# Attention with bucket masks and two expert layers on one core: the first heads' v halves, one conversion and many places moved

## Chip, core and metric

One core of a Trainium2 chip runs the whole program. The metric is device time in microseconds (us) from launch to end of that core. Its engines are TensorE (PE, matmuls; PEld is its weight load), VectorE (DVE), ScalarE (ACT), GpSimd (POOL) and the sync engine (SP), which here only issues transfers (DMAs). A time "of the profile" is measured from the first instruction of one profiled execution.

## What is computed

```python
# q, k, v: (2, 8, 768, 64): 16 heads (h) of 768 rows and 64 columns
q_bucket, k_bucket = bits of (q @ proj > 0), (k @ proj > 0)      # 6 bits each
mask = q_bucket[:, None] == k_bucket[None, :]
scores = where(mask, q @ k.T / 8, -1e9)
attn = softmax(scores);  x = attn @ v                            # -> x: 1536 tokens x 512
h = x @ w_in                     # layer 1: 512 -> 2048
g = (a0 + a1 h + a2 h^2 + a3 h^3) / (1 + |b0||h| + |b1| h^2 + 1e-6)
x = g @ w_out                    # 2048 -> 512
h = x @ w2_in;  out = (h - tanh(h)) @ w2_out                     # layer 2
```

## The kernel before

Numbers of 32 bits are carried through TensorE as two halves (a rounded high part and the rest), so most products are three matmuls. The program has two stages.

The **attention stage** handles 16 heads, each in six chunks j of 128 keys. Per head: `load_qk` brings k and q in one tile (kq); `split_hi` (ScalarE) and `split_lo` (GpSimd, for head 0 VectorE) make the halves A and Bl; `place` and its second part copy them by DMA into the operand tiles TA, TBk and TBq; `bits` multiplies them by the projection (six matmuls in PSUM) and its second part turns the signs into mask rows of TBk and TBq on VectorE, followed by one DMA (head 0 writes both directly). `smax` multiplies for the row maxima, and VectorE reduces them (line 380, mx); `put_max` (head 0: `put_half`, twice) transposes them and sends them as one more row of TBq by DMA. `scores` needs that row: four matmuls (line 498, st), then Exp on ScalarE (e), `round_e` rounds e to 16 bits (eh; `EH_ACT` says how many of 768 columns ScalarE takes, VectorE the rest), `rest_e` subtracts (el; GpSimd, in the last head also VectorE by `EL_DVE_LAST`), and `attend` multiplies eh and el with v (pv). For each pair of heads v is loaded (vraw), its maximum found (`vmax` on VectorE, `vall` on TensorE, "vback" on VectorE, "vagain" on TensorE, `vscale` on VectorE) and each head's v is split into `vhi` (ScalarE) and `vlo` (line 473); `vmean_of` needs both. `normalize` and, for every second head, `to_x` (xT, then xh and xl) write the next stage's input.

Into the last heads the program threads the first eight conversions of the weights (`load_w`, `scale` on ScalarE, `join` on VectorE with two instructions and a PSUM tile "low", `halves` on ScalarE and GpSimd) and the first unit of the expert layer (four `h_mm` with stages a to e).

The **expert stage** then runs on TensorE as a row of 48-matmul blocks: `h_mm` (line 171) and `y_mm` (lines 687, 691) alternately. Its PSUM tiles take over the banks of the attention stage, each as soon as that bank's last user is done.

The order is written out by hand. Every call is entered as a task with a "place"; head h has the base 6h, and a value of the table T, or of EARLY for heads 0 to 3, is added. The tasks are sorted by place and emitted, and **every engine, SP too, runs its instructions in exactly this order**. So a changed number in T matters only where it makes two tasks change sides. The large PSUM tiles (bits, sm, st, xT, low, early h) share three slots of two banks ("double"); the small ones (maxima, v's maximum, mean) share one bank ("single").

Of the kernel before, what the change touches and what calls it, by code (L numbers as in the profile page):

```python
# [10 lines left out]
F32, F32R, F16, I32 = DT.float32, DT.float32r, DT.float16, DT.int32  # L11
AF = mybir.ActivationFunctionType
ALU = mybir.AluOpType
AX = mybir.AxisListType
PSUM = bass.MemoryType.PSUM

B, H, S, D = 2, 8, 768, 64
# [3 lines left out]
P = 128  # L21
NK = S // P
SH = S // 2
# [4 lines left out]
PW = D + 1  # L28


EH_ACT = (768, 768, 384, 768, 512, 768)
ORDERED = ('scalar', 'vector', 'gpsimd', 'tensor', 'sync')
TC_ARGS = dict(schedule_with_timeline_sim=True)
M = dict(a=1, b=3.35, c=3.69, d=5, e=5, y=1.59, scale=3.71, join=3.82, halves=6.35)
EH_ACT_LAST = (0, 0, 768, 0, 384, 0)
EL_DVE_LAST = (128, 0, 0, 128, 256, 384)

EL_DVE = (0, 0, 0, 0, 0, 0)


T = dict(load=-22.01, hi=-15.34, lo=-14.2, place=-13.97, place_a=-13.59, bits=-13.42, bits_out=-12.57,
         put=-3.25, put_out=-3.12, vhi=-6.87, vlo=-4.93, vmean=-2.03, vmean_out=-1.18, lead=9.98, max=0.3,
         exp=0.13, round=0.9, rest=1.95, pv=(5.43, 6.95, 7.43, 8.75, 8.06, 9.23), pv_last=(5.5, 5.5, 7.19,
         8.17, 8.91, 9.32), norm=9.74, x=14.29, x_out=15.02, v=-16.67, vmax=-11.5, vall=-10.2, vscale=-9.9,
         w=-24, w_step=3.88, h0=0.75, slot=0.88, a=0.84, b=2.13, c=2.55, d=4.03, e=4.18, gates=26.99,
         vback=-10.1, vagain=-9.93, w2=-8.0, w2_step=4.0, w_load=6.0)
EARLY = {0: dict(load=-61, hi=-59.04, lo=-59.03, place=-57.89, bits=-57.11, bits_out=-56.82, place_a=-56.45,
                lead=54.43, put=-49.1, v=-59.99, vmax=-57.43, vall=-55.7, vscale=-55.6, vhi=-4.1, vlo=-4.02,
                vmean=-2.21, vmean_out=-1.2, vback=-55.67, vagain=-55.64, put_half=-51.0),
         1: dict(load=-66.5, hi=-64.64, lo=-64.4, place=-61.82, bits=-59.23, bits_out=-58.61, place_a=-57.18,  # L50
                lead=53.53),
         2: dict(load=-64.71, hi=-60, lo=-59.75, place=-59.59, place_a=-59.53, bits=-56.42, bits_out=-56.02,
                lead=9.98, v=-22.32),
         3: dict(load=-20, hi=-15.31, lo=-14.17, place=-14.21, place_a=-13.68, bits=-12.43, bits_out=-11.41,
                lead=9.23)}
NE = 1
T_LAST = dict(norm=9.59, x=10.17, x_out=10.68)


@with_exitstack  # L60
def tile_fn(ctx: ExitStack, tc: tile.TileContext, kq, v, proj, w1i, w1o, a_, b_, w2i, w2o, out):
    nc = tc.nc
# [112 lines left out]
    NCH, NG, FG = 3, 4, 4  # L175
# [66 lines left out]
    with ExitStack() as actx:  # L242
        actx.enter_context(tc.manual_schedule(engines={getattr(nc, e).engine for e in ORDERED}))
        ap = actx.enter_context(tc.tile_pool(name="ap", bufs=1))
# [11 lines left out]
        def halved(x):  # L256
            return x.rearrange("p (n c) ... -> p n c ...", n=2)
# [12 lines left out]
        TAk, TAq, TBk, TBq = {}, {}, {}, {}  # L270
        raw, hilo = {}, {}

        def after(what):

            return nullcontext()
# [8 lines left out]
        praw = ap.tile([P, NB], F32, name="praw")  # L284
# [11 lines left out]
        thr = ap.tile([P, 1], F32, name="thr")  # L296
        amp = ap.tile([P, 1], F32, name="amp")
# [5 lines left out]
        nc.vector.tensor_add(amp, amp, th2)  # L303
        pj = ap.tile([P, P], F32, name="pj")
        nc.vector.memset(pj, 0.0)
        nc.vector.tensor_copy(pj[0:D, 64:70], praw[0:D])
        nc.vector.tensor_scalar(pj[0:D, 70:76], praw[0:D], -1.0, None, op0=ALU.mult)
        nc.vector.tensor_scalar(pj[D:P, 96:102], praw[D:P], -1.0, None, op0=ALU.mult)
        nc.vector.tensor_copy(pj[D:P, 102:108], praw[D:P])
        pj_hi = ap.tile([P, P], F32R, name="pj_hi")  # L310
        pj_lo = ap.tile([P, P], F32R, name="pj_lo")
        nc.vector.tensor_copy(pj_hi, pj)
# [34 lines left out]
        def bits(h):  # L347
            hi, lo = hilo.pop(h)
            ps = double(f"bits{h}")[:, :, 0:SH]
            for x, (l, r) in enumerate(((pj_hi, hi), (pj_lo, hi), (pj_hi, lo))):  # L350
                for n in range(2):
                    nc.tensor.matmul(ps[:, n], l, r[:, n * SH:(n + 1) * SH], start=(x == 0), stop=(x == 2))  # L352

            def out():
                if h == 0:
                    nc.vector.tensor_scalar(halved(TBq[h][64:76]), ps[96:108], thr[96:108], amp[96:108],
                                            op0=ALU.is_gt, op1=ALU.mult)
                    nc.vector.tensor_scalar(halved(TBk[h][64:77]), ps[64:77], thr[64:77], amp[64:77],
                                            op0=ALU.is_gt, op1=ALU.mult)
                    return  # L360
                d = nc.vector.tensor_scalar(halved(TBk[h][64:108]), ps[64:108], thr[64:108], amp[64:108],  # L361
                                            op0=ALU.is_gt, op1=ALU.mult)
                sent.setdefault("thr", d.ins)
                d = nc.sync.dma_start(TBq[h][64:76].bitcast(F32), TBk[h][96:108].bitcast(F32))
                sent.setdefault("bits", d.ins)

            outs["bits", h] = out
# [38 lines left out]
        vraw, vsc, vmx = {}, {}, {}  # L406

        def vsl(h):
            return vraw[h // 2][:, :, (h % 2) * D:(h % 2 + 1) * D]
# [6 lines left out]

        def vmax(pr):
            vmx[pr] = ap.tile([P, 2], F32, name=f"vm{pr}", tag="vm", bufs=2)
            with after("max" if pr else "thr"):
                nc.vector.tensor_reduce(vmx[pr], vraw[pr].rearrange("p t (h d) -> p h t d", h=2),  # L420
                                        axis=AX.XY, op=ALU.max, apply_absolute_value=True)

        nc.vector.memset(pj, 1.0)
        ones2 = pj[0:2]
# [45 lines left out]

        def vlo(h):
            t = VB[h % 3]
            nc.vector.scalar_tensor_tensor(out=t[:, :, D + 1:2 * D + 1], in0=vsl(h), scalar=vsc[h],  # L473
                                           in1=t[:, :, 0:D], op0=ALU.mult, op1=ALU.subtract)

# [44 lines left out]
        pv = {}  # L520
# [72 lines left out]
        def on(place, fn, *args):  # L593
            tasks.append((place, len(tasks), fn, args))

        end, TT = 6 * BH, globals()["T"]
        for h in range(BH):
            g, last = 6 * h, h == BH - 1
            T = {**TT, **EARLY.get(h, {})}
            if h > 0:  # L600
                on(g + T["load"], load_qk, h)
            on(g + T["hi"], split_hi, h)
            on(g + T["lo"], split_lo, h)
            on(g + T["place"], place, h)
            on(g + T["bits"], bits, h)
            on(g + T["place_a"], out_of, "place", h)
            on(g + T["bits_out"], out_of, "bits", h)
            if h:
                on(g + T["put"], put_max, h)
                on(g + T["put_out"], out_of, "put", h)  # L610
            else:
                on(g + T["put_half"], put_half, 0)
                on(g + T["put"], put_half, NK // 2)
            on(g + T["vhi"], vhi, h)
            on(g + T["vlo"], vlo, h)
            on(g + T["vmean"], vmean_of, h)
            on(g + T["vmean_out"], out_of, "vmean", h)
            for j in range(NK):
                on(g + j - T["lead"], smax, h, j)
                on(g + j - T["lead"] + T["max"], out_of, "max", (h, j))  # L620
                on(g + j, scores, h, j)
                on(g + j + T["exp"], out_of, "e", (h, j))
                on(g + j + T["round"], round_e, h, j)
                on(g + j + T["rest"], rest_e, h, j)
                on(g + (T["pv"] if not last else T["pv_last"])[j], attend, h, j)
            t = T if not last else T_LAST
            on(g + t["norm"], normalize, h)
            if h % 2 == 0:
                on(g + T["v"], load_v, h // 2)
                on(g + T["vmax"], vmax, h // 2)  # L630
                on(g + T["vall"], vall, h // 2)
                on(g + T["vback"], out_of, "vback", h // 2)
                on(g + T["vagain"], out_of, "vagain", h // 2)
                on(g + T["vscale"], vscale, h // 2)
            else:
                on(g + t["x"], to_x, h // 2)
                on(g + t["x_out"], out_of, "x", h // 2)
        for n, p in enumerate((f, part) for part in range(2) for f in range(FG)):
            t = end + (TT["w"] + TT["w_step"] * n if n < FG else TT["w2"] + TT["w2_step"] * (n - FG))
            on(t - TT["w_load"], load_w, *p)  # L640
            on(t, W1.scale, *p)
            on(t + 1, W1.join, *p)
            on(t + 2, W1.halves, *p, nc.gpsimd)
        for u in range(NE):
            for fi in range(FG):
                t = end + TT["h0"] + TT["slot"] * (4 * u + fi)
# [74 lines left out]
    for u in range(NU):  # L721
        t = 8 * u
# [68 lines left out]
```

## Time and profile before

| | us |
|---|---|
| median of 3 runs | 786.19 (782.45 to 789.7) |
| the profiled execution, whole | 783.02 |
| its span, first to last instruction | 781.2 |
| TensorE busy | 745.8 (95% of the span) |
| VectorE, GpSimd, ScalarE busy | 525.8, 507.0, 466.2 |

The profile lists each engine's busy time, what ended the idle time before an instruction ("<-"), and the granted clock of TensorE (PEclk; 1.00 is full). A stage in which TensorE is never idle can only be shortened by less work for it; in the others the time hangs on what TensorE waits for.

### The profile page before, as it was taken

What the parts mean: (1) busy time and instruction counts of PE and PEld (TensorE: products, weight loads), DVE (VectorE), ACT (ScalarE), POOL (GpSimd) and SP (SyncE); (2) the same over time, 40 slices, a digit from 0 to 9 for tenths busy, and PEclk for the clock granted to TensorE, in tenths of its full rate; (3) what the DMA queues carried; (4) which work ended last, traced back from release to release, by engine and by line L of the source; (5) the groups of instructions that cost most, each with busy time, mean ns of one, the idle gap of its engine ahead of it and who ended that gap; (6) DMA issues with size and microseconds to landing.
All of it is one profiled execution on the core that took longest, in us unless ns stands there. A gap on an engine that the chain in (4) does not pass through costs nothing.

```text
span 781.2 us, 13222 instructions
## 1 busy us (share of the span) xinstructions
PE 745.8 (95%) x5081; PEld 627.9 (80%) x5081; DVE 525.8 (67%) x820; ACT 466.2 (60%) x756; POOL 507.0 (65%) x395
## 2 busy tenths in 40 slices
PE   4799999999899699999999999999999999999998
PEld 3689888888787588888888888888888888888886
DVE  6678988898879888879899898853322444342222
ACT  2388888878796788777666676764444333332120
POOL 2298898988889687787777778985333434342221
PEclk9999999999999999999999999999999999999999
DMA  6564546447421231121222211221221212200012
GB/s 169 159 164 129 136 135 166 127 112 193 119 77 61 62 101 55 55 80 56 59 76 76 61 54 56 74 86 55 71 64 55 82 54 60 77 27 1 28 41 95
DMA packets 40536, 66.49 MB, mean 85 GB/s; under 512 B 3844, under 2 KB 26468, under 8 KB 40472
## 3 DMA queue, kind: packets, MB, share of 16 engines
q1 hardware_dynamic: 40472, 65.63, 28.8%
q8 instruction: 40, 0.66, 0.4%
q14 instruction: 24, 0.20, 0.1%
HBM read 43.00 MB, written 3.15 MB: 59 GB/s over the span
## 4 chain that ended last, share of the span: by engine, by line
PE 82%; DVE 12%; ACT 2%; issue 2%; DMA 1%; SPq 0%; ACTq 0%; DVEq 0%
PE h L171 32%; PE y L691 17%; PE y L687 17%; PE st L498 6%; DVE mx L380 4%; PE sm L376 3%; PE bits L352 2%; DVE eh L509 1%; PE pv L536 1%; DVE VB L473 1%; PE pv L537 1%; PE pv L539 1%; DVE TBk L361 1%; ACT e L501 1%; DMA vraw<-in_v_dram 1%
## 5 line engine op out<-in xcount | busy, mean ns | idle before, releaser
L239 POOL TENSOR_TENSOR G<-g,G 128x512 fp32r<-128x512 f32 x96 | 123.4, 1295 | 119.5 <-ACT G L234 104.6
L518 POOL TENSOR_TENSOR el<-e,eh 128x768 f16<-128x768 f32 (+2 forms) x96 | 159.1, 1673 | 33.0 <-ACT eh L507 20.2
L171 PE MATMUL h<-xh,wh 128*128 128x512 f32 x368 | 144.0, 391 | 3.6 <-DVE wt L110 3.6
L171 PE MATMUL h<-xl,wh 128*128 128x512 f32 x368 | 143.7, 390 | 0.0
L171 PE MATMUL h<-xh,wl 128*128 128x512 f32 x368 | 143.7, 390 | 0.0
L122 POOL TENSOR_TENSOR wl<-wt,wh 128x512 fp32r<-128x512 f32 x64 | 83.6, 1306 | 71.7 <-ACT wh L121 71.1
L687 PE MATMUL y<-G,wh 128*128 128x512 f32 x384 | 118.3, 389 | 0.0
L691 PE MATMUL y<-wh,G 128*128 128x512 f32 x384 | 118.1, 389 | 0.0
L234 ACT CAST G<-g 128x512 fp32r<-128x512 f32 x96 | 58.3, 619 | 84.9 <-PE y L691 35.7
L501 ACT ACTIVATE e<-st,lnk 128x768 f32<-128x768 f32 x96 | 86.2, 899 | 31.7 <-PE st L498 28.3
L110 DVE SCALAR_TENSOR_TENSOR wt<-wt,low 128x512 int32<-128x512 int32 x64 | 44.0, 687 | 89.5 <-ACT wt L98 85.2
L704 DVE TENSOR_TENSOR ya<-y,ya 128x512 f32<-128x512 f32 x72 | 49.1, 688 | 77.8 <-PE y L691 72.7
L380 DVE TENSOR_REDUCE mx<-sm 128x1 f32<-128x768 f32 x96 | 90.7, 951 | 12.7 <-PE sm L376 10.7
L171 PEld LDWEIGHTS h<-xh,wh 128*128 128x128 f32 x368 | 69.5, 189 | 18.2 <-issue 3.8
L691 PEld LDWEIGHTS y<-wh,G 128*128 128x128 f32 x384 | 72.1, 188 | 14.9
L687 PEld LDWEIGHTS y<-G,wh 128*128 128x128 f32 x384 | 72.1, 188 | 14.9
L209 ACT ACTIVATE s<-h 128x512 f32<-128x512 f32 x48 | 28.5, 598 | 90.4 <-PE h L171 90.3
L171 PEld LDWEIGHTS h<-xh,wl 128*128 128x128 f32 x368 | 69.4, 188 | 14.6
L171 PEld LDWEIGHTS h<-xl,wh 128*128 128x128 f32 x368 | 69.5, 189 | 14.4
L691 PE MATMUL y<-wl,G 128*128 128x512 f32 x192 | 74.7, 389 | 0.0
L687 PE MATMUL y<-G,wl 128*128 128x512 f32 x192 | 74.7, 389 | 0.0
L507 ACT CAST eh<-e 128x768 f16<-128x768 f32 (+2 forms) x92 | 68.1, 740 | 1.5
(122 smaller groups left out, 1603.2 us busy)
## 6 DMA issues: line engine op xcount, KB each, us to landing
raw<-in_w1i_dram SPq DMA_DIRECT2D x16, 512.0 KB
raw<-in_w1o_dram SPq DMA_DIRECT2D x16, 512.0 KB
raw<-in_w2i_dram SPq DMA_DIRECT2D x16, 512.0 KB
raw<-in_w2o_dram SPq DMA_DIRECT2D x16, 512.0 KB
kq<-in_kq_dram SPq DMA_DIRECT2D x16, 384.0 KB
TA<-A SPq DMA_DIRECT2D x32, 192.0 KB
TA<-Bl SPq DMA_DIRECT2D x32, 192.0 KB
vraw<-in_v_dram SPq DMA_DIRECT2D x8, 384.0 KB
```

The source lines that it names most:

```text
L122: lo_eng.tensor_sub(lo, w, hi)
L171: nc.tensor.matmul(ps, l[:, dc], r[:, dc], start=(n == 0), stop=(n == 11))
L234: nc.scalar.copy(gh, live[u, fi])
L239: nc.gpsimd.tensor_sub(gl, live.pop((u, fi)), gt[u, fi])
L380: d = nc.vector.tensor_reduce(mx[h][:, j:j + 1], ps, axis=AX.XY, op=ALU.max)
L498: nc.tensor.matmul(ps[:, n], l[h][0:k, j * P:(j + 1) * P], q[h][0:k, n * SH:(n + 1) * SH], start=(k == P), stop=(k < P))
L501: outs["e", (h, j)] = lambda: nc.scalar.activation(halved(e), ps, AF.Exp, scale=1.0 / math.sqrt(D), bias=lnk)
L507: nc.scalar.copy(eh[h, j][:, 0:n], ef[h, j][:, 0:n])
L518: nc.gpsimd.tensor_sub(el[h, j][:, n:S], e[:, n:S], eh[h, j][:, n:S])
L687: nc.tensor.matmul(ps, l[:, o], r, start=(n == 0), stop=(n == 11))
L691: nc.tensor.matmul(ps, l[:, o], r, start=(n == 0), stop=(n == 11))
L704: nc.vector.tensor_add(ya, ps, ya)
```

## The change

- `vlo` of heads 0 and 1 is done in two steps: ScalarE scales v into a tile of the e ring, GpSimd subtracts. The other heads keep VectorE.
- Head 0's mask rows: the key rows first, then the query rows in two instructions of 384 columns.
- Two of the four small copies that build the projection tile go from VectorE to GpSimd.
- `EH_ACT[2]` 384 to 128: VectorE rounds 640 columns of chunk 2 instead of 384. In the last head ScalarE rounds 640 columns of chunk 4 (384 before) and all of chunk 5 (0 before), and VectorE subtracts 128 of chunk 4 (256 before) and all of chunk 5 (384 before).
- Each of the eight first conversions has its own place (`wt`), and nearly all places change by a little. The distance of the `smax` chunks gets a factor (`ls`; 1.0 but for heads 0 to 2).

```diff
--- before.py
+++ after.py
@@ -28,33 +28,36 @@
 PW = D + 1
 
 
-EH_ACT = (768, 768, 384, 768, 512, 768)
+EH_ACT = (768, 768, 128, 768, 512, 768)
 ORDERED = ('scalar', 'vector', 'gpsimd', 'tensor', 'sync')
 TC_ARGS = dict(schedule_with_timeline_sim=True)
 M = dict(a=1, b=3.35, c=3.69, d=5, e=5, y=1.59, scale=3.71, join=3.82, halves=6.35)
-EH_ACT_LAST = (0, 0, 768, 0, 384, 0)
-EL_DVE_LAST = (128, 0, 0, 128, 256, 384)
+EH_ACT_LAST = (0, 0, 768, 0, 640, 768)
+EL_DVE_LAST = (128, 0, 0, 128, 128, 768)
+
+VLO_POOL = (0, 1)
 
 EL_DVE = (0, 0, 0, 0, 0, 0)
 
 
-T = dict(load=-22.01, hi=-15.34, lo=-14.2, place=-13.97, place_a=-13.59, bits=-13.42, bits_out=-12.57,
-         put=-3.25, put_out=-3.12, vhi=-6.87, vlo=-4.93, vmean=-2.03, vmean_out=-1.18, lead=9.98, max=0.3,
-         exp=0.13, round=0.9, rest=1.95, pv=(5.43, 6.95, 7.43, 8.75, 8.06, 9.23), pv_last=(5.5, 5.5, 7.19,
-         8.17, 8.91, 9.32), norm=9.74, x=14.29, x_out=15.02, v=-16.67, vmax=-11.5, vall=-10.2, vscale=-9.9,
-         w=-24, w_step=3.88, h0=0.75, slot=0.88, a=0.84, b=2.13, c=2.55, d=4.03, e=4.18, gates=26.99,
-         vback=-10.1, vagain=-9.93, w2=-8.0, w2_step=4.0, w_load=6.0)
-EARLY = {0: dict(load=-61, hi=-59.04, lo=-59.03, place=-57.89, bits=-57.11, bits_out=-56.82, place_a=-56.45,
-                lead=54.43, put=-49.1, v=-59.99, vmax=-57.43, vall=-55.7, vscale=-55.6, vhi=-4.1, vlo=-4.02,
-                vmean=-2.21, vmean_out=-1.2, vback=-55.67, vagain=-55.64, put_half=-51.0),
-         1: dict(load=-66.5, hi=-64.64, lo=-64.4, place=-61.82, bits=-59.23, bits_out=-58.61, place_a=-57.18,
-                lead=53.53),
-         2: dict(load=-64.71, hi=-60, lo=-59.75, place=-59.59, place_a=-59.53, bits=-56.42, bits_out=-56.02,
-                lead=9.98, v=-22.32),
-         3: dict(load=-20, hi=-15.31, lo=-14.17, place=-14.21, place_a=-13.68, bits=-12.43, bits_out=-11.41,
-                lead=9.23)}
+T = dict(load=-21.57, hi=-15.42, lo=-15.12, place=-14.05, place_a=-12.96, bits=-13.55, bits_out=-12.65,
+         put=-3.12, put_out=-3.08, vhi=-8.38, vlo=-3.99, vmean=-1.97, vmean_out=-0.81, lead=9.98, max=0.3,
+         exp=0.42, round=0.9, rest=1.38, pv=(5.37, 6.95, 7.8, 8.75, 8.44, 9.16), pv_last=(5.41, 6.77, 8.07,
+         9.01, 8.75, 8.94), norm=9.81, x=14.6, x_out=15.27, v=-16.72, vmax=-11.72, vall=-10.45, vscale=-9.9,
+         h0=0.72, slot=0.93, a=0.84, b=1.9, c=2.24, d=4.03, e=4.17, gates=24.8, vback=-10.25, vagain=-9.92,
+         w_load=6.0, wt=(-41.29, -22.72, -17.84, -12.24, -8.26, -4.0, 0.32, 3.85), ls=1.0)
+EARLY = {0: dict(load=-61.69, hi=-62.14, lo=-60.39, place=-60.58, bits=-58.96, bits_out=-57.68, place_a=-58.4,
+                lead=52.54, put=-46.37, v=-63.23, vmax=-58.62, vall=-56.52, vscale=-54.29, vhi=-6.88,
+                vlo=-6.75, vmean=-5.12, vmean_out=-2.89, vback=-56.49, vagain=-55.68, put_half=-47.77,
+                ls=0.86),
+         1: dict(load=-67.13, hi=-65.44, lo=-65.19, place=-64.04, bits=-59.08, bits_out=-58.81, place_a=-57.52,
+                lead=54.94, ls=1.12),
+         2: dict(load=-64.89, hi=-61.91, lo=-61.61, place=-61.57, place_a=-61.53, bits=-58.68, bits_out=-58.14,
+                lead=9.66, v=-20.61, ls=1.03),
+         3: dict(load=-22.52, hi=-15.52, lo=-14.68, place=-14.44, place_a=-13.73, bits=-12.32, bits_out=-11.43,
+                lead=9.64)}
 NE = 1
-T_LAST = dict(norm=9.59, x=10.17, x_out=10.68)
+T_LAST = dict(norm=9.87, x=10.11, x_out=10.68)
 
 
 @with_exitstack
@@ -303,10 +306,10 @@
         nc.vector.tensor_add(amp, amp, th2)
         pj = ap.tile([P, P], F32, name="pj")
         nc.vector.memset(pj, 0.0)
-        nc.vector.tensor_copy(pj[0:D, 64:70], praw[0:D])
+        nc.gpsimd.tensor_copy(pj[0:D, 64:70], praw[0:D])
         nc.vector.tensor_scalar(pj[0:D, 70:76], praw[0:D], -1.0, None, op0=ALU.mult)
         nc.vector.tensor_scalar(pj[D:P, 96:102], praw[D:P], -1.0, None, op0=ALU.mult)
-        nc.vector.tensor_copy(pj[D:P, 102:108], praw[D:P])
+        nc.gpsimd.tensor_copy(pj[D:P, 102:108], praw[D:P])
         pj_hi = ap.tile([P, P], F32R, name="pj_hi")
         pj_lo = ap.tile([P, P], F32R, name="pj_lo")
         nc.vector.tensor_copy(pj_hi, pj)
@@ -353,10 +356,11 @@
 
             def out():
                 if h == 0:
-                    nc.vector.tensor_scalar(halved(TBq[h][64:76]), ps[96:108], thr[96:108], amp[96:108],
-                                            op0=ALU.is_gt, op1=ALU.mult)
                     nc.vector.tensor_scalar(halved(TBk[h][64:77]), ps[64:77], thr[64:77], amp[64:77],
                                             op0=ALU.is_gt, op1=ALU.mult)
+                    for n in range(2):
+                        nc.vector.tensor_scalar(TBq[h][64:76, n * SH:(n + 1) * SH], ps[96:108, n], thr[96:108],
+                                                amp[96:108], op0=ALU.is_gt, op1=ALU.mult)
                     return
                 d = nc.vector.tensor_scalar(halved(TBk[h][64:108]), ps[64:108], thr[64:108], amp[64:108],
                                             op0=ALU.is_gt, op1=ALU.mult)
@@ -416,9 +420,8 @@
 
         def vmax(pr):
             vmx[pr] = ap.tile([P, 2], F32, name=f"vm{pr}", tag="vm", bufs=2)
-            with after("max" if pr else "thr"):
-                nc.vector.tensor_reduce(vmx[pr], vraw[pr].rearrange("p t (h d) -> p h t d", h=2),
-                                        axis=AX.XY, op=ALU.max, apply_absolute_value=True)
+            nc.vector.tensor_reduce(vmx[pr], vraw[pr].rearrange("p t (h d) -> p h t d", h=2),
+                                    axis=AX.XY, op=ALU.max, apply_absolute_value=True)
 
         nc.vector.memset(pj, 1.0)
         ones2 = pj[0:2]
@@ -470,6 +473,11 @@
 
         def vlo(h):
             t = VB[h % 3]
+            if h in VLO_POOL:
+                x = ap.tile([P, S], F32, name=f"vx{h}", tag="e", bufs=4)[:, 0:SH].rearrange("p (t d) -> p t d", t=NK)
+                nc.scalar.activation(x, vsl(h), AF.Copy, scale=vsc[h])
+                nc.gpsimd.tensor_sub(t[:, :, D + 1:2 * D + 1], x, t[:, :, 0:D])
+                return
             nc.vector.scalar_tensor_tensor(out=t[:, :, D + 1:2 * D + 1], in0=vsl(h), scalar=vsc[h],
                                            in1=t[:, :, 0:D], op0=ALU.mult, op1=ALU.subtract)
 
@@ -616,8 +624,8 @@
             on(g + T["vmean"], vmean_of, h)
             on(g + T["vmean_out"], out_of, "vmean", h)
             for j in range(NK):
-                on(g + j - T["lead"], smax, h, j)
-                on(g + j - T["lead"] + T["max"], out_of, "max", (h, j))
+                on(g + T["ls"] * j - T["lead"], smax, h, j)
+                on(g + T["ls"] * j - T["lead"] + T["max"], out_of, "max", (h, j))
                 on(g + j, scores, h, j)
                 on(g + j + T["exp"], out_of, "e", (h, j))
                 on(g + j + T["round"], round_e, h, j)
@@ -636,7 +644,7 @@
                 on(g + t["x"], to_x, h // 2)
                 on(g + t["x_out"], out_of, "x", h // 2)
         for n, p in enumerate((f, part) for part in range(2) for f in range(FG)):
-            t = end + (TT["w"] + TT["w_step"] * n if n < FG else TT["w2"] + TT["w2_step"] * (n - FG))
+            t = end + TT["wt"][n]
             on(t - TT["w_load"], load_w, *p)
             on(t, W1.scale, *p)
             on(t + 1, W1.join, *p)
```

Whole orders that change by the new places: v of pair 0 is loaded ahead of head 1's kq; head 1's `bits` stand ahead of head 0's first `smax`; the copies of `place(2)` stand ahead of the two `put_half` DMAs on SP; in each pair "vback" stands ahead of the odd head's `vlo`; the first conversion moves from head 12 to head 9; in the last unit the last `join` stands behind stage c of the third early block.

## Rows read from the trace of the kernel before

**Rows 1.** Stages: us, busy us (instructions) of PE, PEld, DVE, ACT, POOL; granted clock.
```profile
0.00:36.60 36.60, 22.41 (x77) 18.47 (x78) 24.07 (x53) 9.30 (x13) 7.87 (x20) 1.00 0.67 174
36.60:186.00 149.40, 143.39 (x1927) 128.28 (x1927) 128.71 (x206) 124.93 (x181) 134.58 (x80) 1.00 0.53 141
186.00:264.40 78.40, 66.94 (x823) 56.68 (x822) 69.36 (x107) 61.54 (x97) 65.49 (x46) 0.95 0.30 86
264.40:776.00 511.60, 511.51 (x2250) 423.50 (x2251) 302.93 (x457) 270.44 (x467) 299.05 (x252) 1.00 0.20 62
```

**Rows 2.** Waits of TensorE over the span: total us, times, longest.
```profile
PE vt L437 <- DVE vdg L434: 6.6, 6, 2.3
```

**Rows 3.** Timeline of the start: start us, us, engine, instruction, [idle before].
```profile
5.78 0.83 ACT L323 CAST A<-kq 128x768 fp32r<-128x768 f32 x1 [1.14 <-DMA kq<-in_kq_dram]
...
6.42 0.90 PE L352 MATMUL bits<-Bl,pj_hi 128*128 128x384 f32 x2
...
7.93 0.95 DVE L420 TENSOR_REDUCE vm<-vraw 128x2 f32<-128x768 f32 x1 [1.68 <-DMA vraw<-in_v_dram]
...
8.92 1.09 DVE L356 TENSOR_SCALAR TBq<-bits,thr,amp 12x768 fp32r<-12x768 f32 x1
...
13.28 1.82 DVE L380 TENSOR_REDUCE mx<-sm 128x1 f32<-128x768 f32 x2 [0.37 <-PE sm L376]
...
15.84 1.08 DVE L361 TENSOR_SCALAR TBk<-bits,thr,amp 44x768 fp32r<-44x768 f32 x1 [0.74 <-PE bits L352]
...
16.95 1.82 DVE L380 TENSOR_REDUCE mx<-sm 128x1 f32<-128x768 f32 x2
...
27.51 1.82 DVE L380 TENSOR_REDUCE mx<-sm 128x1 f32<-128x768 f32 x2
...
30.04 0.74 PE L480 MATMUL vm<-VB,ones 128*128 128x64 f16 x11 [2.33 <-DVE VB L473]
...
30.59 0.99 PE L498 MATMUL st<-TA 128*128 128x384 f32 x2
...
32.08 0.95 DVE L420 TENSOR_REDUCE vm<-vraw 128x2 f32<-128x768 f32 x1 [0.73 <-DMA vraw<-in_v_dram]
...
36.61 0.59 PE L498 MATMUL st<-TA 128*128 128x384 f32 x2
```

**Rows 4.** Timeline around one pair's v maximum, heads 7 and 8.
```profile
112.41 1.65 DVE L473 SCALAR_TENSOR_TENSOR VB<-vraw,vsc,VB 128x384 f16<-128x384 f32 x1
...
115.36 0.38 PE L437 MATMUL vt<-vdg,pj 2*128 2x2 f32 x2 [0.91 <-DVE vdg L434]
...
116.41 0.27 PE L391 MATMUL mt<-ident,mx 128*6 128x128 f32 x1
```

**Rows 5.** Ten microseconds in which two conversions meet head 13; columns as before.
```profile
200.00:205.00 5.00, 3.69 (x25) 2.73 (x21) 4.83 (x10) 3.56 (x7) 3.64 (x3) 1.00 0.75 195
205.00:210.00 5.00, 4.87 (x53) 4.43 (x54) 3.42 (x5) 3.79 (x6) 3.60 (x3) 0.66 0.28 55
```

**Rows 6.** Timeline of the hand-over from the last head to the expert stage.
```profile
241.15 3.13 DVE L509 CAST eh<-e 128x768 f16<-128x768 f32 x2
...
255.55 0.50 PE L171 MATMUL hr<-xh,wh 128*128 128x512 f32 x1 [0.89 <-DVE g L226]
...
261.87 1.02 DVE L576 TENSOR_TENSOR xl<-xT,xh 128x256 fp32r<-128x256 f32 x2 [0.50 <-ACT xh L574]
...
264.26 0.68 DVE L224 SCALAR_TENSOR_TENSOR s<-s,hr 128x512 f32<-128x512 f32 x1
...
264.49 0.77 PE L171 MATMUL h<-xh,wh 128*128 128x512 f32 x1 [3.62 <-DVE wt L110]
...
266.37 0.68 DVE L224 SCALAR_TENSOR_TENSOR s<-s,hr 128x512 f32<-128x512 f32 x1
```

**Rows 7.** By line: ns shortest/median/longest; GpSimd by shape: busy us, mean ns.
```profile
L473 DVE SCALAR_TENSOR_TENSOR VB<-vraw,vsc,VB x16: 610/1088/1858, 29.4 to 223.5; 128x384 f16<-128x384 f32 x16
...
L518 POOL TENSOR_TENSOR el<-e,eh 128x384 f16<-128x384 f32 x1 | 1.0, 1039 | 0.5 <-DVE eh L509 0.5
```

## The prediction

> **What bounds the kernel now.** I read the stages first, then TensorE's waits, then the timeline where the waits are. The stages [rows 1] split the span cleanly. From 264.4 us on TensorE is busy 511.51 of 511.60 us, so nothing the change does to the other engines there can shorten it; what counts is when that stage begins. Before it TensorE idles three times: 14.2 of the first 36.6 us, 6.0 of the next 149.4, 11.5 of the 78.4 before the hand-over. VectorE is the next fullest in the first and third stretch (24.1 and 69.4 us), GpSimd in the second (134.6 of 149.4, 90%). The change can win at most some of these 31.7 us and what a low clock costs there.
>
> The first idle stretch is a chain through VectorE [rows 3]: v of pair 0 lands at 7.9, its maximum, the mask rows, then a row of maxima from 13.28 to 29.33 (27.51 + 1.82), with a pause of 0.74 at 15.84 where TensorE has made `sm` before `bits` of head 1. TensorE's mean of v then waits 2.33 us for `vlo` of head 0, and the first scores start at 30.59. In the second stretch the one repeated wait is "vagain" behind "vback": 6.6 us in six waits, the longest 2.3 in the start, so 4.3 us in the five other pairs [rows 2]. In the third, two conversions meet head 13: 1.44 us idle in ten, and a granted clock of 0.66 in the second half [rows 5]; at the end the expert stage's first matmul waits 3.62 us for the last `join` [rows 6].
>
> All sums are made on the profiled execution, 783.02 us; the median of the runs shown is 786.19, 3.2 above it.
>
> **A. The start: -2.6 us (-0.5 to -4.5).** The two loads change sides: kq of head 1, second in the queue, landed by 5.78; v, third, by 7.93 [rows 3]. I give v about 6.2 and kq1 7.9. VectorE can then take the maximum of v before the last `bits` product of head 0 ends at 7.32. The key rows cost about 1.09 as the query rows did (8.92); a half of 384 columns lies between 0.55 and 1.09, I take 0.7. So the mask rows end near 10.0 (7.5 + 1.1 + 1.4) and not at 11.1, and `bits` of head 1, now ahead of the first `smax`, runs from about 10.9 to 12.9 in a gap of TensorE. Its second part (1.08) is done near 14.1, and the first maximum comes then, later than 13.28; but the third comes near 15.95 where it came at 16.95: -1.0. From there ten maxima at 0.91, two small rescalings (an estimate, 0.3 each) and one 1.08 make 10.8 us of work that took 12.4 (16.95 to 29.33). The head-1 maxima interleaved with head 0's leave TensorE ahead, so I leave 0.6 of the 1.6 us of waits: another -1.0, end at 27.35. Head 0's `vlo` is then no VectorE work: GpSimd needs about 1.04 us for that shape [rows 7], ScalarE hardly more (an estimate, its 768 columns took 0.83 at 5.78), both long before; that removes the 2.33 us wait, and the first scores could come 3 to 4 us earlier. What is late next is pair 1's v: it landed at 32.08, its issue stands behind head 2's mask DMA on SP, and that moves by about 2.7 to 2.9 us. The rest of the start hangs on its maximum. So -2.6 arrives, -4.5 would be the scores' own shift, and -0.5 what is left if the waits only move. On SP the six copies of `place(2)` now stand ahead of the two maxima rows of head 0, which the first scores need; this costs nothing as long as head 2's halves are ready, covered by the 4 us the scores gain; without this cover A falls to -0.5.
>
> **B. Five pairs: -3.2 us (0 to -4.3).** In the old order `vlo` (1.65 at 112.41) runs between v's maximum and "vback", and TensorE loses 0.91 at 115.36 [rows 4]; the new one puts it after "vback". "vback" comes about 1.4 us earlier and TensorE does not wait there. But the transpose `mt` (116.41) uses the bank that `vscale` reads, and `vscale` now stands behind `vlo`: "vback" near 113.9, `vlo`, then `vscale`, which lies between 115.36 and 116.41 in the old order, so half a microsecond. With `vlo` at its median of 1.09 [rows 7], `mt` could start near 115.6, TensorE is there at about 115.5, and some 0.2 of the 0.86 a pair comes back. So 0.65 times 5. With the shortest `vlo`, 0.61, all 0.86 is won; with 1.86, under 0.2.
>
> [...]
>
> **C. The first conversion, now in head 9: +0.5 us (0 to +1.4).** Its two VectorE instructions take 1.37 us together (between the end of xl at 262.89 and 264.26 [rows 6]). VectorE idles 20.7 of 149.4 us in this stretch [rows 1], 1.9 a head, so the work fits in, but it also takes one of three PSUM slots. I take a third.
>
> **D. Two conversions less one at head 13: -1.6 us (0 to -3.1).** [...]
>
> **E. The hand-over: +1.2 us (-2.4 to +2.1).** In the last head VectorE loses one 768-wide rounding (3.13 for two, so 1.56 [rows 6]) and two thirds of another, and gets more subtraction; I count -1.3. Its chain thus releases the early h at 255.55 sooner, by at most the 0.89 that TensorE waited there; so xl ends at about 262.0. But the last `join` (1.37) now stands behind three instructions of stage c, which take 2.11 (264.26 to 266.37). If the same PSUM bank holds its tile, the first expert matmul is released 2.11 later than the chain: -0.9 + 2.1 = +1.2. It was released by just that `join` before, and the three slots rotate; the slot of xT is free first in the new order too. Gone is its cover: nothing else delays TensorE there.
>
> **At nothing.** The 256 columns more on VectorE in each head cost about a quarter of a microsecond and fall into its 1.9 us of idle time a head; without that, up to 3.5 in 14 heads, which is in the bounds of B. The two small copies on GpSimd run beside VectorE's (plus or minus 0.3 us). Head 1's `vlo` adds 1.04 to GpSimd, behind its first subtraction; TensorE uses that only several chunks later.
>
> **Sum.** -2.6 - 3.2 + 0.5 - 1.6 + 1.2 = -5.7, so 777.3 on the profiled execution and 780.5 on the median. I say 778.
>
> **The rivals.** (1) *Another bank at the hand-over*: by then a second slot, that of the third early h, has come free, and if the last `join` gets it, TensorE waits only for xl: 264.49 becomes 262.0, -2.4 and not +1.2, so -9.3 in all, 773.7. For it: the new order frees that slot just before the `join`. Against: the slot of xT has been free longer. (2) *The gains are given back before the hand-over*: VectorE and GpSimd are 86% and 90% busy in the second stretch [rows 1]; if TensorE outruns them, B and half of A turn into new waits: -5.7 + 3.2 + 1.3 = -1.2, 781.8. For it: GpSimd's 90% and C; against: TensorE's 96%. (3) *Slower: the low clock lasts longer*. A pair of score matmuls takes 0.99 at 30.59 and 0.59 at 36.61 [rows 3], so TensorE works at half rate until then, though the granted column reads 1.00; it rose after TensorE had been busy from 30.04 on. If the new order, with its scores split by the wait for pair 1's v, keeps TensorE below that for longer, each microsecond beyond about 34 costs half of one. It decides against the change from 11.4 us on (at 45 us); two heads longer (some eleven heads fill the 149.4 us, so 13.5 each) cost 13.5, 790.8. For it: the hole at 29 to 30; against: afterwards TensorE is as full as before.
>
> [...]
>
> **Chances.** My forecast 0.50, rival 1 0.22, rival 2 0.17, rival 3 0.11. About 1% (7.8 us) is what a measurement of this kernel can tell from no change. Faster by over 1%: rival 1 and a third of the forecast's spread, 0.39. Slower by over 1%: most of rival 3, 0.09. Within: 0.52. The range, 771 to 786, holds the forecast and rivals 1 and 2 on either base; below it lie the far ends of A, B and D together, above it rival 3. The forecast's own range is 774 to 783.
>
> **What would show it.** A: the mean of v no longer waits; first scores near 27, pair 1's v landing near 29, the pairs of matmuls at 0.59 from 34 on. B: no "vagain" wait, at most 0.3 at `mt`. C: a wait of TensorE on a `join` in head 9. D: no stretch below 1.00 between 190 and 230 us. E: the first expert matmul released by the last `join`, some 3 us behind xl; if by xl, rival 1. Wrong it is if the start of the last stretch has not moved by 4 to 8 us, or if that stretch is not full.

## The result and the profile after

The changed kernel takes 776.27 us (median of 4 runs, 775.36 to 777.76), the kernel before 784.87 (4 runs, 782.45 to 789.7): a ratio of 0.9886, 95% interval 0.9848 to 0.9924. The forecast was 778.0 with 771 to 786. Profile against profile it is 777.76 against 783.02, 5.3 us, where the sum said 5.7. These two executions are not typical: 783.02 lies 3.4 to 3.7 us below the medians of the later runs of before (786.46 to 786.73, see the experiments), and 777.76 is the slowest of the four of after. By the medians the change is 8.6 us, or some 10 against those later runs. So the forecast time came out and the gain is larger than the sum; this section and the next ask what became of its parts.

Where TensorE waits after the change (us in total, times, longest):

```profile
PE bits L355 <- DVE pj_hi L315: 5.2, 1, 5.2
PE h L174 <- DVE g L229: 4.2, 1, 4.2
PE st L506 <- DVE wt L113: 3.3, 2, 2.6
PE vt L440 <- DVE vdg L437: 2.7, 1, 2.7
PE vt L432 <- DVE vm L423: 2.5, 1, 2.5
```

The "vagain" row of [rows 2] has one wait left, that of the start: the five others are gone. The hand-over waits longer than before, 4.2 us, and for another releaser than in [rows 6]. Two waits of about 2.5 us are new: for the maximum of pair 1's v, and for a `join` in the last head.

The start, timeline (start, duration, engine, instruction, idle before it):

```profile
6.41 0.94 DVE L423 TENSOR_REDUCE vm<-vraw 128x2 f32<-128x768 f32 x1
...
8.68 1.29 DVE L362 TENSOR_SCALAR TBq<-bits,thr,amp 12x384 fp32r<-12x384 f32 x2
...
25.32 0.55 PE L488 MATMUL vm<-VB,ones 128*128 128x64 f16 x12
25.79 0.61 PE L506 MATMUL st<-TA 128*128 128x384 f32 x2
...
29.07 0.95 DVE L423 TENSOR_REDUCE vm<-vraw 128x2 f32<-128x768 f32 x1 [1.36 <-DMA vraw<-in_v_dram]
30.17 0.27 PE L432 MATMUL vt<-ident,vm 128*2 128x128 f32 x1 [2.54 <-DVE vm L423]
30.19 0.59 PE L506 MATMUL st<-TA 128*128 128x384 f32 x2
...
32.71 0.99 PE L506 MATMUL st<-TA 128*128 128x384 f32 x2
...
43.61 0.59 PE L506 MATMUL st<-TA 128*128 128x384 f32 x2
```

The first scores start 4.8 us earlier than in [rows 3], at 25.79 and at once at 0.61 a pair. Then TensorE stands for 2.54 us until the maximum of pair 1's v is there. The first pair behind that hole still takes 0.59 (30.19), the next 0.99 again (32.71). The granted clock in windows (PE busy is the first pair of numbers, the clock the third number from the end):

```profile
28.00:32.00 4.00, 1.83 (x8) 1.41 (x8) 1.44 (x4) 3.24 (x5) 2.80 (x3) 0.84 0.63 223
32.00:36.00 4.00, 4.00 (x13) 3.52 (x13) 3.57 (x7) 2.87 (x6) 3.51 (x3) 0.50 0.02 4
36.00:40.00 4.00, 4.00 (x41) 3.63 (x41) 2.04 (x4) 3.00 (x5) 3.70 (x3) 0.50 0.55 141
40.00:44.00 4.00, 4.00 (x41) 3.84 (x39) 2.73 (x3) 1.85 (x4) 2.48 (x2) 0.88 0.64 157
```

TensorE is full from 32 to 44, but at a granted clock of 0.50 until 40 and a mean of 0.88 from there to 44. So the scores that began early lose most of their lead within head 0.

The best way to see where time went is the start of each head's first Exp, read from the timelines and set against the kernel before's own (us, negative is earlier; e8 to e12 are experiments, below):

| kernel | head 0 | 1 | 4 | 5 | 8 | 10 | 12 | 14 | last chunk of 15 |
|---|---|---|---|---|---|---|---|---|---|
| before, at | 32.3 | 43.8 | 82.9 | 96.7 | 137.1 | 164.1 | 191.7 | 221.7 | 241.9 |
| after | -5.4 | -0.8 | -1.7 | -3.0 | -3.9 | -4.0 | -3.6 | -6.4 | -5.4 |
| e8, pairs alone | -0.7 | -1.1 | +0.1 | -0.9 | -1.6 | -2.3 | -3.1 | -4.9 | -4.9 |
| e9, bank alone | -0.9 | +2.8 | +2.5 | +2.5 | +2.8 | +2.8 | +2.8 | +2.8 | +3.4 |
| e10, pairs and bank | -0.1 | -0.4 | -0.5 | -0.6 | -0.8 | -1.5 | -2.3 | -4.5 | -3.0 |
| e11, start and bank | -5.3 | -2.2 | -1.9 | -2.1 | -1.8 | -1.8 | -1.8 | -3.3 | -2.4 |
| e12, start, pairs, bank | -5.4 | -2.1 | -1.9 | -3.0 | -3.6 | -4.4 | -6.0 | -7.7 | -7.0 |

Each row is one execution, and what is left of the lead in head 1 differs among executions with the same start: 0.8 us in after, 1.5 to 3.4 in e4 to e7, e11 and e12. e9 has the start of before and is 2.8 us later there.

The hand-over of after, timeline:

```profile
255.63 1.02 DVE L584 TENSOR_TENSOR xl<-xT,xh 128x256 fp32r<-128x256 f32 x2 [0.50 <-ACT xh L582]
...
258.01 0.75 DVE L229 SCALAR_TENSOR_TENSOR g<-g,na,hr 128x512 f32<-128x512 f32 x1
...
258.81 0.80 PE L174 MATMUL h<-xh,wh 128*128 128x512 f32 x1 [4.22 <-DVE g L229]
259.39 0.69 DVE L113 SCALAR_TENSOR_TENSOR wt<-wt,low 128x512 int32<-128x512 int32 x1
```

The first expert matmul waits neither for xl (done at 256.65) nor for the last `join` (done at 260.08), but for stage c of the third early block. From there on TensorE is full, as in the last row of [rows 1]:

```profile
258.80:770.00 511.20, 511.19 (x2247) 423.11 (x2248) 302.08 (x456) 270.55 (x467) 298.79 (x252) 1.00 0.19 62
```

The stage starts 5.7 us earlier than before (258.81 for 264.49) and the span is 5.2 shorter.

### The profile page after: what moved, and what is told of

Its sections match the earlier page's. It is cut to its first block, busy times and chain, and to the rows that moved or that the text cites. A ratio compares the mean times of both kernels' runs of the same rounds, so it can differ in the third digit from the quotient of the medians.

```text
span 776.0 us, 13230 instructions
## 1 busy us (share of the span) xinstructions
PE 747.1 (96%) x5081; PEld 627.7 (81%) x5081; DVE 526.9 (68%) x816; ACT 467.3 (60%) x759; POOL 511.0 (66%) x398
## 4 chain that ended last, share of the span: by engine, by line
PE 88%; DVE 6%; ACT 2%; DMA 2%; issue 1%; SPq 0%; POOL 0%; ACTq 0%; DVEq 0%; POOLq 0%
PE h L174 33%; PE y L699 17%; PE y L695 17%; PE st L506 7%; PE sm L380 4%; PE bits L355 2%; PE pv L544 2%; PE hr L174 2%; PE pv L545 2%; PE pv L547 2%; ACT e L509 1%; DVE mx L384 1%; DVE eh L517 1%; DVE TBk L365 1%; PE vm L488 1%
## 5 line engine op out<-in xcount | busy, mean ns | idle before, releaser
L526 POOL TENSOR_TENSOR el<-e,eh 128x768 f16<-128x768 f32 (+1 forms) x95 | 159.1, 1687 | 25.6 <-ACT eh L515 14.9
L515 ACT CAST eh<-e 128x768 f16<-128x768 f32 (+2 forms) x93 | 65.8, 708 | 1.9
```

The costliest lines, as they stand in the source:

```text
L515: nc.scalar.copy(eh[h, j][:, 0:n], ef[h, j][:, 0:n])
L526: nc.gpsimd.tensor_sub(el[h, j][:, n:S], e[:, n:S], eh[h, j][:, n:S])
```

## Experiments

Twelve kernels, in three groups that each ran beside the kernel before (medians 786.70, 786.73 and 786.46 there, of 19 to 23 runs). e1 to e4 take one thing back in the changed kernel or alter it, e5 and e6 concern the hand-over, e7 to e12 put single parts on the kernel before.

### e1: pair 1's v loaded early

```diff
-                lead=9.66, v=-20.61, ls=1.03
+                lead=9.66, v=-62.5, ls=1.03
```

> The changed kernel, but the load of pair 1's v is issued on SP ahead of head 2's copies and of the two rows of head 0's maxima, so that it lands before the maxima of head 1 are done (it landed at about 29 us; the wait of TensorE for it is 2.5 us at 30.2). Theory 1 (the start hangs on this landing, and the hole of 2.5 us is also what lets TensorE's clock fall to the lower level from about 31 to 41 us): the wait goes, the granted clock stays at 1.00 there, and some 10 us at half rate give back up to 5; the kernel takes 770 to 773 us against 776.3. Theory 2 (VectorE or ScalarE bound the first heads, the clock costs nothing there): only part of the hole goes, at most 1 us, 775 to 776.5.

Measured: 780.82 us, ratio 0.9922 (0.9895 to 0.9948): slower than after. The maximum of v is there in time, and the hole stays:

```profile
27.70 0.95 DVE L423 TENSOR_REDUCE vm<-vraw 128x2 f32<-128x768 f32 x1
28.60 1.01 PE L506 MATMUL st<-TBq,TBk 77*128 77x384 f32 x2 [2.24 <-DMA TBq<-mr]
```

Ahead of the row of maxima in SP's queue, the load delays that row (SP begins to issue it at 22.97 us, at 21.97 in after), and the scores wait for it instead. So the edit tested neither theory: the hole has moved and is hardly shorter. In the two profiles xl ends at the same time (256.51, in after 256.65), and the 3.4 us between their spans come from the hand-over: its wait is 7.6 us here and 4.2 in after, though nothing near it was changed. The medians lie 4.6 us apart; the rest of that is open.

### e2: `vlo` of heads 0 and 1 back on VectorE

```diff
-VLO_POOL = (0, 1)
+VLO_POOL = ()
```

> The changed kernel with the lower halves of v of heads 0 and 1 back on VectorE, nothing else. Theory 1 (pair 1's v is what the start waits for): VectorE is idle between about 27.5 and 29.1 us anyway, the first scores come some 0.6 to 2 us later, but the scores after pair 1's maximum hardly move, at most 0.5 us; 776 to 777 us. Theory 2 (the move to ScalarE and GpSimd is what made the start shorter): the exponentials of head 2 come 1.5 to 2.5 us later than in the changed kernel; 778 to 779 us.

Measured: 778.79, ratio 0.9909 (0.9877 to 0.9942), 2.5 us above after by the medians; the ranges of the runs overlap (776.56 to 779.96, in after 775.36 to 777.76). The mean of v waits again:

```profile
28.71 0.75 PE L488 MATMUL vm<-VB,ones 128*128 128x64 f16 x11 [2.64 <-DVE VB L481]
```

The hand-over is that of after (4.2 us for the same `g`), so the difference is of the start: the heads' Exp come 4.1 us later in head 0, but only 1.1 to 1.2 us from head 6 to head 11, and the two spans differ by 0.3. So the edit counts, by 2.5 us at most; the hole behind it takes the rest of its gain.

### e3: the pairs' places back, e4: the first conversion back

```diff
-vhi=-8.38, vlo=-3.99 ... vmax=-11.72, vall=-10.45 ... vback=-10.25, vagain=-9.92
+vhi=-8.38, vlo=-4.93 ... vmax=-11.5, vall=-10.2 ... vback=-10.1, vagain=-9.93     # e3
-wt=(-41.29,
+wt=(-24.0,                                                                       # e4
```

> The changed kernel with five places of the v preparation as before, so that the odd head's lower half stands on VectorE between v's maximum and the back step again, in every pair. Theory 1 (term B): the waits of TensorE on the back step return, about 0.86 us in each of five pairs, and the kernel loses 2.5 to 4.3 us: 779 to 780.5 us. Theory 2 (other engines would have used up the gain): 776 to 777.5 us, with the waits moved to other instructions.

e3 measured: 786.53, ratio 1.0011 (0.9982 to 1.0041): the whole gain is gone, more than either theory said. TensorE's "vagain" row:

```profile
PE vt L440 <- DVE vdg L437: 11.9, 7, 2.7
```

It is more than [rows 2] had: among the other new places "vagain" stands one block of `attend` earlier, and a wait is 1.57 us at 114.56, not 0.91; behind several of them the granted clock falls (0.72 at 85 to 90 us, 0.69 at 140 to 145). So e3 is not a clean undo, and its size says little about B; that the waits return with the order does.

> The changed kernel with the first conversion of weights back at its old place in head 12. Theory 1 (in head 9 it costs nearly 2 us, in head 12 it costs about as much and pulls the clock down): heads 9 to 11 are 1.5 to 2 us earlier than in the changed kernel, heads 12 to 13 lose 2 to 3.5, in all 0 to +1.7: 776 to 778 us. Theory 2 (it costs nothing in head 9, the loss there has another cause): heads 9 to 11 do not move, and the kernel is 2 to 3.5 us slower, 778 to 780 us.

e4 measured: 777.13, ratio 0.9898 (0.9856 to 0.9939), about after's time. By the heads' Exp the two differ much: from head 8 to the last chunk of head 11 e4 gains 3.2 us on after, in head 12, where the conversion now stands, it loses 2.2 again, and the first expert matmul waits 5.6 us, for the last `join`, instead of 4.2. So a conversion in head 9 costs more than one in head 12, and the hand-over hid it.

### e5, e6: a bank of its own at the hand-over

The first expert tile of unit 1 takes the bank of the later y products in place of one of the three shared slots; e6 is e4 with the same edit.

```diff
+    def first_h(u, fi):
+        if (u, fi) == (1, 0):
+            return yps.tile([P, 512], F32, name=f"h{u}_{fi}", tag="y")[:, 0:CT]
+        return bank("h")(u, fi)
-    scratch.update(h=bank("h"), r0=bank("r0"),
+    scratch.update(h=first_h, r0=bank("r0"),
```

> The changed kernel, but the first expert matmul block of unit 1 writes into the bank that the first y block uses later (free since the last head's normalisation) and not into a bank of the early h blocks. Theory 1 (the 4.2 us wait at the hand-over is for that bank; x itself is ready about 2.1 us earlier): the block starts right behind the last xl, the wait of 4.2 becomes about 2.1 and the kernel takes 774 to 774.5 us against 776.3; the following blocks find their banks free. Theory 2 (the other banks, or weights, or the y block that shares the bank, bind next): the gain moves into a wait of the second h block or of the first y block, and the kernel stays at 776 to 776.5.

> The changed kernel with both the first conversion at its old place in head 12 and the free bank for the first expert block. Theory 1 (the two add up: the conversion costs 3 us in head 9 and 2 in head 12, and at the hand-over the wait of 5.6 us that this order has falls to about 2): 771 to 773 us. Theory 2 (the conversion's move was worth something in the changed kernel and only the start differed by chance): 774 to 776 us.

Measured: e5 774.19, ratio 0.9858 (0.9825 to 0.9891), 2.1 below after; e6 776.02, ratio 0.9890 (0.9850 to 0.9931). In e5 the first tile now waits for xl only, and the second for the `g` that the first waited for:

```profile
255.94 0.50 PE L174 MATMUL h<-xl,wh 128*128 128x512 f32 x1 [0.44 <-DVE xl L584]
...
258.65 0.56 PE L174 MATMUL h<-xh,wh 128*128 128x512 f32 x1 [1.97 <-DVE g L229]
```

The hand-over is thus decided by who held the slot. In e6 the second tile waits 3.38 us, for the last `join`: the conversion's place, in head 12 or 9, has changed the holder again, and e6 is 1.8 us slower than e5.

### e7, e8: the start alone, the pairs alone

e7 is the changed code with the old T, rounding shares and conversions, and the new EARLY; e8 is the kernel before with five numbers of the pairs, from pair 2 on.

```diff
-vlo=-4.93 ... vmax=-11.5, vall=-10.2 ... vback=-10.1, vagain=-9.93
+vlo=-3.99 ... vmax=-11.72, vall=-10.45 ... vback=-10.25, vagain=-9.92           # e8
```

> The kernel before with only the start changed: the places of heads 0 to 3, the two-step lower halves of v of heads 0 and 1, the mask rows of head 0 in this order and the small copies. Theory 1 (term A): the exponentials from head 2 on come 2 to 4 us earlier than before, and this stays to the end: 2 to 4 us less than the kernel before. Theory 2 (the gain depends on the later places, since VectorE falls behind): under 1 us at the end.

> The kernel before with only the five places of the v preparation from pair 2 on as in the change. Theory 1 (term B, 0.65 us in each of five pairs): 3 to 4 us less than the kernel before. Theory 2 (the run that took these places away from the changed kernel lost 9 us, so they are worth that much): 7 to 9 us less. Theory 3 (no gain without the other places): under 1 us.

Measured: e7 787.08, ratio 1.0021 (0.9990 to 1.0052); e8 786.53, ratio 1.0006 (0.9975 to 1.0036). Neither part alone gains anything (the second theory of e7, the third of e8). But e8's Exp starts drop by about 1 us at each pair from head 4 on and stand at -4.9 in the last head (table above), with no "vagain" wait left but the start's. All of it goes at one place: from the end of xl to the last instruction e8 takes 523.1 us, the kernel before 518.3. Among TensorE's waits of e8:

```profile
PE h L171 <- DVE g L226: 7.8, 1, 7.8
```

The first expert matmul now waits for the last early block, 4.1 us longer than for the `join` of [rows 6]. e7 has the same wait (7.7; its profiled execution took 792.24 us, the slowest of its ten). No tile of the shared slots changed its order in e8: its edits move only v's preparation, whose tiles lie elsewhere.

### e9 to e12: the same parts with the hand-over's bank

The edit of e5 on the kernel before (e9), on e8 (e10), on e7 (e11), and on both parts together (e12).

> The kernel before with one edit: the first expert tile of the second unit takes the bank of the later y products instead of one of the three shared slots, so that its first matmul waits for xl and not for the tile that happened to hold its slot. Theory 1 (the hand-over is decided by which tile holds the slot, 3.62 us of wait in the trace of before): the first product is released by xl, about 1.4 us earlier than by the join, its matmuls run in the time that was idle, and the whole is 1 to 2.5 us shorter than the kernel before: 784 to 785.5 where before takes 786.5. Theory 2 (the wait only moves to the next tile): no difference, 786 to 787.

> The five pairs' places alone on the kernel before, plus the bank of its own for the first expert tile. Without that bank the profile showed 4.9 us gained by the last head and all of it lost in a hand-over wait of 7.8 us for the last early block. Theory 1 (the pairs are worth about 1 us each and the hand-over hid it): 4 to 6 us below the kernel with the bank alone, 779 to 781.5. Theory 2 (the gain is lost anyway, since the early blocks end no sooner): within 1.5 us of the kernel with the bank alone, 783.5 to 787.

> The start's new places and head 0's and 1's lower halves of v by ScalarE and GpSimd on the kernel before, plus the bank of its own for the first expert tile. Without that bank: 2 to 3.6 us ahead until head 5, then given back in waits for the mask rows' DMA and the low clock behind them, and a hand-over wait of 7.7 us. Theory 1 (term A is worth 2 to 3 us and the rest hid it): 781.5 to 783.5. Theory 2 (given back before the hand-over): within 1.5 us of the kernel with the bank alone, 783.5 to 787.

> The start and the five pairs together on the kernel before, plus the bank of its own for the first expert tile. The whole change with that bank took 774.2. Theory 1 (start and pairs add up, and are most of the change): 776 to 779. Theory 2 (the other places are what keeps the gain): 781 to 785.

| | median, us | ratio to before | second expert tile waits for | end of xl to last instruction, us |
|---|---|---|---|---|
| e9, bank alone | 783.75 | 0.9967 (0.9941 to 0.9993) | last `join`, 1.40 | 515.7 |
| e10, pairs | 782.86 | 0.9959 (0.9931 to 0.9987) | last early block, 5.53 | 520.6 |
| e11, start | 783.89 | 0.9956 (0.9932 to 0.9981) | last early block, 5.54 | 520.0 |
| e12, start and pairs | 774.38 | 0.9839 (0.9809 to 0.9869) | last `join`, 1.40 | 515.9 |

e10 lies between its two theories, e11 in the range of the second, e12 below both. One part gives 0.9 us or none, both give 9.4. The reason stands in the last two columns. Hand-over of e10, then of e12:

```profile
260.46 0.69 DVE L110 SCALAR_TENSOR_TENSOR wt<-wt,low 128x512 int32<-128x512 int32 x1
...
264.61 0.75 DVE L226 SCALAR_TENSOR_TENSOR g<-g,na,hr 128x512 f32<-128x512 f32 x1
...
265.42 0.79 PE L171 MATMUL h<-xh,wh 128*128 128x512 f32 x1 [5.53 <-DVE g L226]
```

```profile
257.09 0.69 DVE L114 SCALAR_TENSOR_TENSOR wt<-wt,low 128x512 int32<-128x512 int32 x1
...
257.92 0.47 PE L175 MATMUL h<-xh,wh 128*128 128x512 f32 x1 [1.40 <-DVE wt L114]
...
261.25 0.75 DVE L230 SCALAR_TENSOR_TENSOR g<-g,na,hr 128x512 f32<-128x512 f32 x1
```

Here VectorE does the same work in the same order; only the instruction that frees the tile's slot differs, and the waits with it by 4.1 us. An estimate: without these 4.1 us, e10 would be 5.0 below e9 and e11 4.0 below it, 9.0 together, against 9.4 measured. By the last column, which also holds what comes behind the wait (in after, behind 4.22 us, a granted clock of 0.50 from 260 to 262 and 0.80 from 262 to 264), 4.9 and 4.3 come off, and it is 5.8 and 4.2, 10.0 together. The same sum without the bank: e8 would be 4.3 below the kernel before and e7 3.7 (both with 4.1 taken off). So the pairs are worth 4 to 6 us and the start about 4, by medians; the intervals leave each 2 to 3 us either way. e12 takes the same time as e5 (774.38 and 774.19): with the bank, everything else in the change, conversions, rounding shares and the rest of the places, is together worth nothing that these runs can tell.

## Why the prediction was right, step by step

**The bound: right.** The last stage is full and just starts earlier, by 5.7 us; all was decided before it.

**A, the start (-2.6, from -0.5 to -4.5): the mechanism half right, the size within its bounds.** The mean of v no longer waits and the scores start at 25.79 (I said near 27); v of pair 1 is read at 29.07 (I said 29). That the pairs of matmuls are at 0.59 from 34 on was wrong: they are from about 41 on. Rival 3 had the place and the kind: the hole splits the scores, and behind it a pair takes 0.99 again (32.71), at a granted clock of 0.50. It did not decide, since the pairs were short earlier (0.61 at 25.79), and the delay stayed below its point of 45 us. In head 4 after stands at -1.7, e11 and e12 at -1.9; by the medians the start is worth about 4. The profiled execution of before was 3.4 to 3.7 us below the medians of its later runs. e9, whose start has before's order, has a mean granted clock of 0.987 in its profiled execution, where before has 0.992, and its heads from head 1 to head 14 come 2.5 to 2.8 us late; a start of that kind in other runs of before would explain the difference, but I have no trace of one. On record is that the clock goes with it: of the 62 runs of before beside the experiments, the 13 with a mean granted clock below 0.980 have a median of 788.6 us, the 41 with 0.985 or more one of 785.2. So part of what the start is worth by the medians may be a low clock that it avoids; the two were not separated.

**B, the pairs (-3.2, 0 to -4.3): right in mechanism, too small.** The term that was mis-sized is `vlo` "at its median of 1.09". Behind "vback" it mostly takes 0.60. GpSimd and VectorE around one pair (before, after, and one late pair of after):

```profile
111.99 1.65 POOL L518 TENSOR_TENSOR el<-e,eh 128x768 f16<-128x768 f32 x1
```

```profile
109.37 1.65 POOL L526 TENSOR_TENSOR el<-e,eh 128x768 f16<-128x768 f32 x1 [0.37 <-ACT eh L515]
...
110.96 0.60 DVE L481 SCALAR_TENSOR_TENSOR VB<-vraw,vsc,VB 128x384 f16<-128x384 f32 x1
111.07 2.01 POOL L526 TENSOR_TENSOR el<-e,eh 128x768 f16<-128x768 f32 x1
...
164.44 1.65 POOL L526 TENSOR_TENSOR el<-e,eh 128x768 f16<-128x768 f32 x1 [0.35 <-POOL el L526]
164.55 1.95 DVE L481 SCALAR_TENSOR_TENSOR VB<-vraw,vsc,VB 128x384 f16<-128x384 f32 x1
```

In before, `vlo` runs from 112.41 to 114.06 [rows 4], and the subtraction of GpSimd in which it begins ends at 113.64. In after it runs from 110.96 to 111.56, and that subtraction ends at 111.02; at the late pair it is 166.50 and 166.09. All 206 `vlo` of the 14 traces follow one line. Where GpSimd's instruction has more than 0.3 us left when `vlo` begins (119 of them), `vlo` ends 0.41 to 0.42 us after it; where it has at most 0.1 us left or GpSimd is idle (62), `vlo` takes 0.60 to 0.62. So its length is what is left of that instruction and 0.42 us, but no less than 0.60. The new order starts it late in one, so it is short, and nearly the whole wait of 0.86 is won: in e12 against e11 the five pairs gain 0.7 to 0.9 us each, 4.1 together, in after the first three 1.1 to 1.3 each. The pair at 164.55 begins with a subtraction, and `mt` waits 0.74 there: the price that I gave for a long `vlo`.

GpSimd's instruction is longer too where it begins inside a `vlo`: the subtraction at 111.07 takes 2.01 us and the one at 109.37 1.65. So what I took for a constant, 1.09, is not one: in before it goes from 0.61 to 1.86 [rows 7] with the rest of the other's instruction.

**C (+0.5, 0 to +1.4): wrong in size.** e4 and e6, against after, give 3.2 us each, from head 8 to the last chunk of head 11. The step that failed is "VectorE idles 1.9 us a head, so the work fits in". The two instructions push the next pair's preparation by enough that `vlo` begins with a subtraction (1.95 at 164.55; 0.60 in e4), and `mt` waits. TensorE's waits between 148 and 168 sum to 1.8 us in after, to 0.1 in e4; where the rest of the 3.2 goes is not shown. No wait on a `join` appears in head 9.

**D (-1.6, 0 to -3.1): no run shows this term as it stands.** What the runs show in its place: after has no stretch below 1.00 between 190 and 230, as I said, and taking the first conversion out of head 12 saves 2.2 us (e4, e6). But the fall of the clock at 205 to 210 [rows 5] is absent from e8, e10, e11 and e12 too (1.00 there), which leave the conversions where they were; it is present in e9 (0.82). So it does not hang on where the first conversion stands; what caused the fall stays open.

**E (+1.2, -2.4 to +2.1): the wrong tile.** The chain did come 0.83 us earlier against the last Exp (20.15 us from its start to xl's end, 20.98 before; I said 0.9). But "if the same PSUM bank holds its tile" failed: the slot was the third early block's, freed at 258.76, a case between my forecast and rival 1. From xl to the first matmul it is 2.16 us where it was 1.60: +0.56 and -0.83, so -0.3 and not +1.2. Nearest to rival 1's case, release by xl, is e5, though its second tile still waits 1.97: 2.1 us better than after.

**At nothing.** The 256 columns more cost VectorE more than the quarter of a microsecond that I gave: its two roundings of a head take 1.38 us before (means 0.92 for 384 columns, 0.46 for 256) and 2.07 after (0.84 for 640, 1.22 for the other, which still has 256). No wait of TensorE grew by it that I can name, and e12, with the old shares, takes the time of e5.

**Rival 2** shows in one execution only. In e7 TensorE, 2 us ahead, meets in head 5 a mask row that its DMA has not yet brought (1.36 us at 99.29), and the granted clock falls to 0.51 in the next three microseconds; nothing is left of the lead. But that trace is of the slowest of e7's runs. e11, in the same order up to the hand-over, waits 0.95 us at this place (98.82), its clock stays at 1.00, and it is still 1.8 us ahead in head 12. In e12, with the pairs, the wait is gone. So what hid each part alone is the hand-over and not rival 2.

So the right total is in part luck. It rests on errors that cancel: A and B larger than forecast, C larger, E better, and an unforeseen hole in the start. And the 778 that I said lies between the sum on the profiled execution, 777.3, and that on the median, 780.5; against the medians, the sum of -5.7 was too small by some 3 us or more.

## What to carry to other kernels

Where a stage's first tile takes over a shared PSUM slot, read which instruction frees it before sizing anything else: here it was worth 4 us and changed with edits that touch none of its instructions, so that two parts of some 4 us each showed nothing alone; give that tile a bank of its own and then measure the parts. Where a VectorE instruction's length follows GpSimd's, as `vlo`'s does here, let it begin late in a GpSimd instruction, not behind its start. An early start of TensorE can lose part of its lead where a wait splits it: here the scores came 5.4 us earlier, and behind a hole of 2.5 us and 9 us at a granted clock of 0.50 (31 to 40, in after) 0.8 to 2.2 were left in head 1 (after, e5, e7, e11, e12).

## What the runs showed that was not expected

- The holder of the first expert tile's slot, over all kernels: the last `join` (before 3.6, e3 5.6, e4 5.6 us), the third early block (after and e2 4.2), the last early block (e1 7.6, e7 7.7, e8 7.8). How the slots are given out is not in a trace, and why e8 changes it stays open.
- The length of one `vlo` shape, 0.60 to 2.02 us, is the rest of the GpSimd instruction in which it begins and 0.42 us, at least 0.60 (above).
- The granted column of before reads 1.00 at 30.59, while a pair of matmuls takes 0.99 [rows 3]; in after it reads 0.50 for the same 0.99. In the start the durations are the safer sign.
